# The last chunk's down projection: three float32r products of exact parts in place of seven float32 block products

## The chip, the cores and the metric

One NeuronCore of a Trainium2 chip runs the whole program. The metric is the device time of one execution in microseconds (us). Engines are named as in the profile: PE does the matmuls (PEld its weight loads), DVE, ACT and POOL are the vector, scalar and GpSimd engines, SP issues most of the DMAs. Each engine takes its instructions strictly in the order in which the kernel's Python emits them.

## The reference

An mLSTM cell runs over 768 steps of 4 batches and 8 heads of size 40; its output, laid out as 3072 tokens by 320 values, goes through a feed-forward block with an exact GELU. Cut to what matters here:

```
x = attn_out.transpose(0, 2, 1, 3).reshape(B * S, H * D)   # 3072 x 320
h = x @ w_in                                               # 320 x 2048
g = 0.5 * h * (1.0 + erf(h / sqrt(2)))
out = g @ w_out                                            # 2048 x 320
```

The weights come as float64 and everything is computed in float32.

## The kernel before

The sequence is cut into six chunks of 128 steps (`c` = 0 to 5). A chunk is 4 batches of 128 tokens, so 512 tokens. For each chunk there is the cell (scores, carried state, values), an up projection (`up`), and a down projection (`down_steps`). For c = 1 to 4 the down projection of chunk c is interleaved with the cell of chunk c+1, in an order written out by hand (the string `DOWN`: each `F` is one step of 16 matmuls of the down projection, other letters are steps of the cell). The last chunk, c = 5, has no cell beside it: its `up` and then its 14 `F` steps run alone.

**Up projection (L839 to L905).** The 2048 hidden values are 16 tiles `f` of 128; `HF` = 8, and tile f = 8e+i is named by e (0 or 1) and i. The product x·w_in is made of three float32r products: hi·hi, lo·lo and all·mid, where `w_in_hi`, `w_in_lo`, `w_in_mid` and `x_hi`, `x_lo`, `x_all` are exact parts of the factors (L703 to L720, L744 to L764); `PART` = 1 - 2^-13 and `BASE` = 1 + 2^-12 make the parts. The moving operand is 512 tokens wide. `pair(f)` (L845) makes two tiles i for both e, 24 matmuls over the first 256 rows of x, and `rest(u)` (L864) adds the last 64 rows for two pairs, 24 matmuls. The order is pair 0, pair 1, rest 0, pair 2, pair 3, rest 1. Pairs 0 and 2 write the PSUM buffers `h`,`h`,`a`,`a`; pairs 1 and 3 write `tr`,`tr`,`b`,`b`. `out` (L874) takes GELU on ACT from PSUM into `g`.

The parts hi and lo of w_in stay in SBUF; mid is summed anew in every chunk by `join_weight` (L762). Its results lie in two rings: joins 1, 4, 6 and 9 in the ring `pow` (two buffers, of which `T[4]`, a sum of w_out blocks, holds one from chunk 1 to its last use), the others in the ring `w_in` (12 buffers, of which the ten `w_in_lo` hold ten). Where a ring has no free buffer, the writer waits until the last reader of the oldest one is done. In `up`, DVE has these in order: joins 0, 1 (pair 0), 3, 4, 2 (pair 1), 5, 6, then, during pairs 2 and 3, 8, 9 and 7, between the sums of `hidden_sums`.

**Down projection (L934 to L999).** It is a Strassen-like scheme with seven block products in float32: blocks of 8 hidden tiles, 256 tokens and 160 output columns. `w_out` is held in SBUF as [128, 16, 320]; one block of it, `w_out[:, 0:8, 160:]`, is overwritten in chunk 1 by a difference of blocks (`weight_sum(3)`, `T[3]`), and `w_sums0`, `w_sums1` and `T[4]` hold further sums. Sums of `g` blocks are made by `hidden_sums` (L787) and, in the last chunk, `sum_late` (L974), both on DVE. Each product is 2 steps (token tiles t) of `HF` matmuls per tile, 128x128 weights and 160 moving columns; `p1` to `p7` evict them. The two products with `k == 3` have a bank for each token tile in the last chunk. `send` (L907) writes 128 tokens to DRAM in two DMAs; in the last chunk one of the two goes on ACT's queue.

**Buffers.** `const`, `raw`, `two`, `outp`, `wts`, `parts` (`fars[0]`) are SBUF pools, `gp` holds `g`, `ps_tr`, `ps_h`, `ps_mm` are PSUM pools of two buffers a tag. Tiles of one pool and tag share its buffers in turn.

Of the kernel before, what the change touches and what calls it, by code (L numbers as in the profile page):

```python
# [16 lines left out]
P = 128  # L17
# [19 lines left out]
DOWN = """  # L37
# [5 lines left out]
def kernel(  # L43
# [52 lines left out]

    w_out = const.tile([P, NF, DM], F32, name="w_out")
    ident = const.tile([P, P], F32, name="ident")  # L100
    e_hi = const.tile([P, 1], F32, name="e_hi")
    e_lo = const.tile([P, 1], F32, name="e_lo")
# [2 lines left out]
    ewT = const.tile([P, NCH - 1, BH], F32, name="ewT")  # L105
    gT = const.tile([P, NCH - 1, BH], F32, name="gT")
    dec = const.tile([P, NCH - 1, B * NP], F32, name="dec")
    state = [const.tile([P, NP, 2 * D1], F32, name=f"state{b}") for b in range(B)]
    blocks = const.tile([P, 2, H, DP], F32, name="blocks")
    qb = [blocks[:, n] for n in range(2)] + [const.tile([P, H, DP], F32, name="qb2")]  # L110
    by_block = blocks.rearrange("p n h d -> p (n h d)").rearrange("p (m i x) -> p m i x", m=NP, i=2)
    kb = [const.tile([P, H, DP], F32, name=f"kb{n}") for n in range(NQ)]
    vb = [const.tile([P, H, D1], F32, name=f"vb{n}") for n in range(NQ)]
    shared = lambda shape, dt, name: wts.tile(shape, dt, name=name, tag="hi", bufs=5)
    W = {n: shared([P, H, L], F32, f"W{n}") for n in range(B - 1)}
    qk = shared([P, 2, H, DP], F32, "qk")
    qb.append(qk[:, 0])
    kb.append(qk[:, 1])
    vb.append(shared([P, H, D1], F32, "v3"))
    ob = [const.tile([P, DM], F32, name=f"ob{n}") for n in range(NLD)]  # L120
    y_rest = const.tile([P, 2, R], F32, name="y_rest")
    last = gates.tile([P, P], F32, name="last")
    eye = gates.tile([P, P], BF16, name="eye")
# [2 lines left out]
    i_sb = gates.tile([BH, NCH, L], F32, name="i_sb")  # L126
    kq_d = [dram.tile([B, 2, H * L, D], F32, name=f"kq{c}_d") for c in range(2, NCH)]
    M_d = dram.tile([NCH - 1, BH, L], F32, name="M_d")
    swapped_d = [dram.tile([P, n, BH], F32, name=f"swapped{n}") for n in (NCH - 2, NCH - 3)]

    def out_of(n):
# [25 lines left out]
    def copy_chunk(c, batches=range(B)):  # L157

        for b in batches:
            for i, src in enumerate((k, q)):  # L160
                for hip in range(2):
                    nc.sync.dma_start(out=kq_d[c - 2][b, hip].rearrange("(m i x t) d -> i x m (t d)", m=NP, i=2, x=16)[i],
                                      in_=src[b, hip::2, c * L:(c + 1) * L, :].rearrange("m (x t) d -> x m (t d)", x=16))
# [572 lines left out]
    def products_begin():  # L736

        gate_ctx.close()
        pool = ctx.enter_context(tc.tile_pool(name="parts", bufs=1))
        w_sums.extend(pool.tile([P, HF, HD], F32, name=f"w_sums{n}") for n in range(2))  # L740
        parts["x_all"] = pool.tile([P, NX + 1, TG], F32R, name="x_all")
        fars.extend([pool])

# [18 lines left out]
    def join_weight(i):  # L762
        w_mid[i] = raw.tile([P, 2, WP // 2], F32R, name="w_in_mid", tag="pow") if i % 5 in (1, 4) else w_f(F32R, "w_mid")
        nc.vector.tensor_tensor(out=w_mid[i], in0=w_hi[i], in1=w_lo[i], op=OP.add)  # L764
# [22 lines left out]
    def hidden_sums(g, f0, f1):  # L787

        (a11, a21), (_, a22) = [[g.t[:, HF * e + f0:HF * e + f1, HT * h:HT * (h + 1)] for h in range(2)]
                                for e in range(2)]  # L790
        s1, s2 = [t[f0 // (HF // 2)][:, f0 % (HF // 2):f0 % (HF // 2) + f1 - f0, :] for t in (g.s1, g.s2)]
        nc.vector.tensor_tensor(out=s1, in0=a21, in1=a22, op=OP.add)  # L792
        nc.vector.tensor_tensor(out=s2, in0=s1, in1=a11, op=OP.subtract)
        nc.vector.tensor_tensor(out=a21, in0=a11, in1=a21, op=OP.subtract)
# [41 lines left out]

    def up(g, sums_too, turns):  # L839

        def split_to(i):
            while len(w_lo) <= i:
                split_weight()

        def pair(f, ahead):  # L845

            at = [f // 2 * 5 + f % 2 * 3 + x for x in range(NX)]
            split_to(at[1])
            for i in at:
                if i not in w_mid:  # L850
                    join_weight(i)
            pus = [[pool.tile([P, TG], F32, name="pu", tag=tag) for e in range(2)]
                   for pool, tag in (((ps_h, "h"), (ps_mm, "a")), ((ps_tr, "tr"), (ps_mm, "b")))[f % 2]]
            ahead()
            mid = [w_mid.pop(i) for i in at]
            for n, (w, x) in enumerate((([w_hi[i] for i in at], parts["x"]), ([w_lo[i] for i in at], parts["x_lo"]), (mid, parts["x_all"]))):
                for i in range(2):
                    for e in range(2):
                        for k in range(NX):
                            nc.tensor.matmul(in_pairs(pus[i][e]), w[k][:, e, i * P:(i + 1) * P], in_turns(x[:, k, :]),  # L860
                                             start=(n == 0 and k == 0), stop=False, skip_group_check=True)
            return pus

        def rest(u, banks, order):  # L864
            mid = w_mid.pop(5 * u + 2)
            for i in order:
                pu = banks[i]
                for n, (w, x) in enumerate(((w_hi[5 * u + 2], parts["x"]), (w_lo[5 * u + 2], parts["x_lo"]), (mid, parts["x_all"]))):
                    for e in range(2):
                        r = halves[e]  # L870
                        nc.tensor.matmul(in_pairs(pu[e]), w[r, i // 2, i % 2 * P:(i % 2 + 1) * P], in_turns(x[r, NX, :]), start=False,  # L871
                                         stop=(n == 2), skip_group_check=True)

        def out(i, e, pu):  # L874
            nc.scalar.activation(out=g.t[:, HF * e + i, :], in_=pu[e], func=AF.Gelu, scale=4097.0)  # L875

        if c == 1:
            copy_chunk(2, range(1, B))
        b0 = pair(0, lambda: split_to(4))
        b1 = pair(1, lambda: join_weight(2))  # L880
        for step in turns[:1]:
            step()
        while later_loads:
            later_loads.pop(0)()
        if c == 1:
            copy_chunk(3)
        rest(0, b0 + b1, (0, 1, 2, 3))
        split_to(6)
        join_weight(5)
        join_weight(6)  # L890
        for i, pu in enumerate(b0 + b1):
            for e in range(2):
                out(i, e, pu)
        for step in sums_too[:5]:
            step()
        b2 = pair(2, lambda: split_to(9))
        hidden_sums(g, 0, 2)
        b3 = pair(3, lambda: (hidden_sums(g, 2, 4), join_weight(7)))
        for step in turns[1:] + sums_too[5:]:
            step()  # L900
        rest(1, b2 + b3, (2, 3, 0, 1))
        for i, e in ((2, 0), (2, 1), (3, 0), (0, 0), (1, 0), (3, 1), (0, 1), (1, 1)):
            out(4 + i, e, (b2 + b3)[i])
        hidden_sums(g, HF - 2, HF)
        hidden_sums(g, HF - 4, HF - 2)  # L905
# [28 lines left out]
    def down_steps(c, g):  # L934
# [3 lines left out]

        def product(lhs, rhs, k, first, t, then):

            own = k == 3 and c == NCH - 1
            at, n, i = ((k, t), 1, 0) if own else (k, 2, t)
            if first and i == 0:
                bank[at] = ps_mm.tile([P, n, HD], F32, name="po", tag="a" if own else "b")
            for j in range(HF):

                nc.tensor.matmul(bank[at][:, i, :], lhs(j, t), rhs(j), start=(first and i == 0 and j == 0),  # L947
                                 stop=(i == n - 1 and j == HF - 1), skip_group_check=True)
            if own:
                then(bank[at], slice(t, t + 1))  # L950
            elif t == 1:
                then(bank[at])

        def block(h, n):
            if h not in o_sb:
# [12 lines left out]

        def p2(pb):
            nc.scalar.copy(out=block(0, 0), in_=pb)  # L970
            if c == NCH - 1:
                sum_late()

        def sum_late():  # L974
            for i in range(2):
# [3 lines left out]
        def p5(pb):  # L979
            add(block(1, 1), pb, block(1, 0))  # L980

        def p7(pb, tiles=slice(0, 2)):
            add(block(1, 1)[:, tiles], pb, block(1, 1)[:, tiles])

        def p3(pb):
            add(block(0, 1), pb, block(1, 0))
            for t in range(2):
                send(c, t, o_sb[0][:, t, :])

        def p4(pb, tiles=slice(0, 2)):  # L990
            add(block(1, 0)[:, tiles], pb, block(1, 0)[:, tiles])
            for t in range(2)[tiles]:
                send(c, 2 + t, o_sb[1][:, t, :])

        todo = ((A(0, 0), Bm[0][0], 0, True, p1), (Sm(g.s2), T[2], 1, True, p6),
# [39 lines left out]
    steps |= cell_steps(0, "mwgtscvyx") | cell_steps(1, "MWGTSCVYXR")  # L1035
    play(FRONT, steps)
    for c in range(1, NCH):
        g, later, steps = Hidden(True), [], {}
        if c + 1 < NCH:
            steps = cell_steps(c + 1, "MWGTscVYXRLKQDCBSjh", g)  # L1040
        up(g, weight_sum(1) + weight_sum(2) + weight_sum(3) if c == 1 else [], [lambda b=b: (steps["K"](b), steps["Q"](b)) for b in range(2)] if steps else [])
        if c == 1:
            later = weight_sum(4)
        products, late = down_steps(c, g)
        steps |= dict(F=in_turn(products), Z=in_turn(later), N=late)
        play("F " * 14 if c + 1 == NCH else DOWN, steps)


# [28 lines left out]
```

## Time and profile before

| | us |
|---|---|
| median of three runs | 470.47 (469.64, 470.47, 470.61) |
| the profiled execution, its own time | 470.64 |
| span of that execution | 468.8 |
| PE busy | 458.0 (98%) |
| DVE busy | 319.9 (68%) |
| ACT busy | 238.1 (51%) |
| last chunk's up projection on PE | 408.19 to 434.68 |
| last chunk's down projection on PE | 434.68 to 465.32 |

The span is from the first to the last instruction; the execution's own time is 1.8 us longer. "PEclk", the granted clock, is 1.00 in all of the stretches used here. An instruction's busy time includes its start and its drain, so that consecutive ones overlap: what an engine pays for one of many is the distance from start to start, read from the timeline, and not the mean of its busy time.

### The profile page before, as it was taken

Reading aid. Unit: us, or ns where it says so; the run is one execution under the profiler, and the core shown is the slowest. Engines: PE = TensorE matmul, PEld = TensorE weight load, DVE = VectorE, ACT = ScalarE, POOL = GpSimd, SP = SyncE. Lnnn points to the kernel's source line nnn. Section 1 sums busy time; section 2 is a strip of 40 time slices with the busy share of each in tenths; the row PEclk is TensorE's granted clock in tenths of the full one; section 3 lists DMA queues with packets and bytes.
Section 4 is the critical chain, followed back from the end, with each engine's and each line's share of the span. In section 5 each row is a group of like instructions: output and inputs, shape, how many; then the busy total and the mean of one; then the engine's idle time right before and its main releaser. Section 6 shows DMA issues by size and latency. Waiting matters only on the chain.

```text
span 468.8 us, 12989 instructions
## 1 busy us (share of the span) xinstructions
PE 458.0 (98%) x5380; PEld 406.4 (87%) x5380; DVE 319.9 (68%) x694; ACT 238.1 (51%) x517; POOL 79.8 (17%) x120
## 2 busy tenths in 40 slices
PE   8899999999999999999999999999999999999996
PEld 7787788867788899988898988899988899988996
DVE  7799879798878996746576645586646657624320
ACT  6886999954354684203783213684203883222300
POOL 3002120000020232300433200443203213000000
PEclk9899999999999999999999999999999999999999
DMA  9997993367876740067981056980059830100001
GB/s 174 190 198 178 201 232 87 86 127 202 142 189 121 116 80 3 24 117 154 196 131 17 22 119 141 209 133 14 30 79 216 121 78 1 37 23 0 1 1 56
DMA packets 172795, 49.80 MB, mean 106 GB/s; under 512 B 154720, under 2 KB 166272, under 8 KB 172736
## 3 DMA queue, kind: packets, MB, share of 16 engines
q1 hardware_dynamic: 172416, 48.64, 51.3%
q8 instruction: 42, 0.69, 0.6%
q10 hardware_dynamic: 320, 0.33, 0.2%
q14 instruction: 17, 0.14, 0.1%
HBM read 44.82 MB, written 9.37 MB: 116 GB/s over the span
## 4 chain that ended last, share of the span: by engine, by line
PE 87%; DVE 7%; DMA 2%; issue 1%; SPq 1%; ACT 1%; DVEq 0%
PE po L947 31%; PE pu L860 22%; PE po L924 7%; PE pu L871 6%; PE pu L805 5%; PE ph L656 3%; PE ps L554 2%; PE ps L538 2%; PE px L696 2%; PE pu L811 2%; PE pf L609 1%; DMA kb<-in_k_dram 1%; PE pf L620 1%; SPq L170 1%; PE pt L516 1%
## 5 line engine op out<-in xcount | busy, mean ns | idle before, releaser
L947 PE MATMUL po<-w_out,g 128*128 128x160 f32 x640 | 94.2, 302 | 0.0
L875 ACT ACTIVATE g<-pu 128x512 f32<-128x512 f32 x80 | 40.3, 620 | 98.3 <-PE pu L871 98.3
L947 PEld LDWEIGHTS po<-w_out,g 128*128 128x128 f32 x640 | 87.8, 190 | 2.5 <-ACT g L875 1.7
L947 PE MATMUL po<-w_sums,sums 128*128 128x160 f32 x320 | 45.9, 302 | 0.0
L947 PEld LDWEIGHTS po<-w_sums,sums 128*128 128x128 f32 x320 | 43.8, 190 | 0.4
L466 ACT ACTIVATE W<-W,aT 128x128 f32<-128x128 f32 x128 | 39.2, 389 | 2.0 <-POOL W L440 1.9
L860 PE MATMUL pu<-x_hi,w_in_hi 128*128 128x512 f32 x160 | 39.0, 386 | 0.0
L440 POOL TENSOR_SCALAR_AFFINE_SELECT W<-W 128x1024 f32<-128x1024 f32 (+2 forms) x20 | 24.7, 1245 | 81.6 <-DMA W<-M_d 81.1
L860 PE MATMUL pu<-x_lo,w_in_lo 128*128 128x512 f32 x160 | 37.8, 379 | 0.0
L924 PE MATMUL po<-w_out,g 128*128 128x320 f32 x128 | 35.2, 433 | 0.0
L960 DVE TENSOR_TENSOR o_sb<-po,o_sb 128x320 f32<-128x320 f32 (+1 forms) x27 | 12.5, 465 | 32.8 <-PE po L947 28.8
L860 PEld LDWEIGHTS pu<-x_hi,w_in_hi 128*128 128x128 f32 x160 | 29.6, 189 | 5.6 <-ACT g L875 1.7
L792 DVE TENSOR_TENSOR sums<-g 128x512 f32<-128x512 f32 x20 | 16.4, 820 | 26.5 <-ACT g L875 26.5
L860 PEld LDWEIGHTS pu<-x_lo,w_in_lo 128*128 128x128 f32 x160 | 30.2, 189 | 4.3
L525 POOL TENSOR_TENSOR vw<-vb,ewT 128x328 f32<-128x328 f32 x12 | 9.9, 837 | 137.8 <-DMA vb<-in_v_dram 97.8
L685 ACT COPY y_rest<-ob 128x128 f32<-128x128 f32 x16 | 4.8, 298 | 54.9 <-DVE ob L678 29.2
L924 PEld LDWEIGHTS po<-w_out,g 128*128 128x128 f32 x128 | 24.0, 190 | 9.6
L764 DVE TENSOR_TENSOR w_in_mid<-w_in_hi,w_in_lo 128x512 fp32r<-128x512 f32 x20 | 13.7, 687 | 24.4 <-PE pu L860 24.4
L860 PE MATMUL pu<-x_all,w_mid 128*128 128x512 f32 x80 | 30.3, 379 | 0.0
L860 PE MATMUL pu<-x_all,w_in_mid 128*128 128x512 f32 x80 | 30.3, 379 | 0.0
L805 PE MATMUL pu<-first_x,w_in 128*128 128x256 f32 x128 | 29.2, 382 | 0.6 <-DVE w_in L387 0.6
L805 PEld LDWEIGHTS pu<-first_x,w_in 128*128 128x128 f32 x128 | 23.8, 190 | 4.3 <-DVE w_in L387 1.0
(183 smaller groups left out, 879.3 us busy)
## 6 DMA issues: line engine op xcount, KB each, us to landing
W<-M_d SPq DMA_DIRECT2D x16, 512.0 KB, 5.5
bits<-in_moe_w_in_dram SPq DMA_DIRECT2D x20, 256.0 KB, 4.3
bits<-in_moe_w_out_dram SPq DMA_DIRECT2D x16, 320.0 KB, 3.2
blocks<-kq_d SPq DMA_DIRECT2D x32, 128.0 KB, 3.3
ob<-in_o_gate_dram SPq DMA_DIRECT2D x24, 160.0 KB, 3.9
out_dram<-o_sb SPq DMA_DIRECT2D x36, 80.0 KB, 2.0
kq_d<-in_k_dram SPq DMA_DIRECT2D x32, 80.0 KB, 2.6
kq_d<-in_q_dram SPq DMA_DIRECT2D x32, 80.0 KB, 2.4
```

The source lines that it names most:

```text
L440: nc.gpsimd.affine_select(out=x, in_=x, compare_op=OP.is_ge, fill=1.0e30, base=base, pattern=[[0, H], [1, x.shape[2]]], channel_multiplier=-1)
L466: nc.scalar.activation(out=W[n][:, h, :], in_=src, func=AF.Exp, scale=-1.0, bias=aT[:, self.c, r:r + 1])
L656: nc.tensor.matmul(ph[r, h, :], Pm[:, h, r], vb[turn_of(n)][:, h, :], start=True, stop=True)
L764: nc.vector.tensor_tensor(out=w_mid[i], in0=w_hi[i], in1=w_lo[i], op=OP.add)
L792: nc.vector.tensor_tensor(out=s1, in0=a21, in1=a22, op=OP.add)
L805: nc.tensor.matmul(banks[-1][e][:, i - i0, :], in_tile(i, x)[:, e, i % 2 * P:(i % 2 + 1) * P], first_x[:, x, t0:t1], start=(x == 0 and i = ...
L860: nc.tensor.matmul(in_pairs(pus[i][e]), w[k][:, e, i * P:(i + 1) * P], in_turns(x[:, k, :]), start=(n == 0 and k == 0), stop=False, skip_g ...
L871: nc.tensor.matmul(in_pairs(pu[e]), w[r, i // 2, i % 2 * P:(i % 2 + 1) * P], in_turns(x[r, NX, :]), start=False, stop=(n == 2), skip_group ...
L875: nc.scalar.activation(out=g.t[:, HF * e + i, :], in_=pu[e], func=AF.Gelu, scale=4097.0)
L924: nc.tensor.matmul(po[b], g.t[:, f, b * L:(b + 1) * L], w_out[:, f, :], start=(f == 0), stop=(f == NF - 1))
L947: nc.tensor.matmul(bank[at][:, i, :], lhs(j, t), rhs(j), start=(first and i == 0 and j == 0), stop=(i == n - 1 and j == HF - 1), skip_grou ...
L960: nc.vector.tensor_tensor(out=to, in0=pb, in1=x, op=OP.add)
```

## The change

The last chunk leaves the seven block products. A class `LastDown` forms, as the up projection does, three float32r products with the full width of 320 output columns: 4 token tiles, 16 hidden tiles and 3 kinds of part (hi, lo, all·mid). The parts of `w_out` are made in the last `up`: `weights` (hi, on ACT), `weights_lo` and `weights_mid` (on DVE). The parts of the hidden values are made per tile: `gelu` into a scratch tile, `split_hi` (ACT), `split_lo` (two DVE instructions). All of them lie in buffers that the last cell and the earlier chunks no longer use. The hidden tiles come in two rounds of eight (pairs 0 and 1; pairs 3 and 2). Since `w_out[:, 0:8, 160:]` is overwritten in chunk 1, that block is stored to DRAM before that, and loaded again in chunk 4 after `p7`, the last reader of the difference. The tags added to existing tiles only give the names by which their buffers are shared. Sums of `g` and `sum_late` are no longer made in the last chunk, and the special case `own` of `product` goes.

```
+    right_d = dram.tile([P, DFF // P // 2, DM // 2], F32, name="right_d")
...
+        ROUNDS = ((0, 8, 1, 9, 2, 10, 3, 11), (6, 14, 7, 15, 4, 12, 5, 13))
...
+            self.groups = [(0, 4, part(fars[0], "w_sums0", 4)), (8, 4, part(fars[0], "w_sums1", 4))]
+            singles = [part(const, f"{x}{n}") for x, m in (("ob", NLD), ("vb", NQ), ("state", B)) for n in range(m)]
+            singles += [part(two, "vw") for _ in range(2)] + [part(fars[0], "hs", bufs=2) for _ in range(2)]
+            triples = [part(wts, "W", 3) for _ in range(NW)]
+            singles += [x for t in triples for x in cut(t)]
+            self.groups += [(f, 1, singles.pop(0)) for f in (4, 12, 5, 13, 6, 14, 7, 15)]
...
+        def weights(self, f, n, to):
+            nc.scalar.activation(out=to, in_=w_out[:, f:f + n, :].rearrange("p f d -> p (f d)"), func=AF.Copy, scale=PART * 2.0 ** -12)
+        def weights_lo(self, f):
+            nc.vector.scalar_tensor_tensor(out=self.lo[f], in0=self.hi[f], scalar=-BASE * 2.0 ** 12, in1=w_out[:, f, :], op0=OP.mult, op1=OP.add)
+        def weights_mid(self, f):
+            if self.w_mid is None:
+                self.w_mid = const.tile([P, NF, DM], F32R, name="w_out_mid", tag="w_out")
+            nc.vector.tensor_tensor(out=self.w_mid[:, f, :], in0=self.hi[f], in1=self.lo[f], op=OP.add)
...
+        def gelu(self, f, pu):
+            n = len(self.whole) % HF
+            if n < 2:
+                if n == 0:
+                    self.two = const.tile([P, 2, TG], F32, name="g_whole", tag="blocks")
+                self.whole[f] = self.two[:, n, :]
+            else:
+                pool, tag = ((raw, "sig"), (outp, "o_sb"))[n // 2 % 2]
+                self.whole[f] = pool.tile([P, TG], F32, name="g_whole", tag=tag)
+            nc.scalar.activation(out=self.whole[f], in_=pu, func=AF.Gelu, scale=4097.0)
+        def split_hi(self, f):
...
+            nc.scalar.activation(out=self.b[f], in_=self.whole[f], func=AF.Copy, scale=PART)
+        def split_lo(self, f):
+            nc.vector.scalar_tensor_tensor(out=self.b_lo[f], in0=self.whole[f], scalar=-1.0 / BASE, in1=self.b[f], op0=OP.mult, op1=OP.add)
+            nc.vector.tensor_tensor(out=self.all[:, f, :], in0=self.whole[f], in1=self.b[f], op=OP.subtract)
+        def products(self):
+            po = [pool.tile([P, DM], F32, name="po", tag=tag) for pool, tag in ((ps_tr, "tr"), (ps_mm, "b")) for _ in range(2)]
+            part = lambda f: ((self.b[f], self.hi[f]), (self.b_lo[f], self.lo[f]), (self.all[:, f, :], self.w_mid[:, f, :]))
+            first, last = (self.ROUNDS[0][0], 0), (self.ROUNDS[1][-1], 2)
+            for n, ts in ((0, range(B)), (1, (0, 1)), (1, (2,)), (1, (3,))):
+                for k in range(3):
+                    for t in ts:
+                        for f in self.ROUNDS[n]:
+                            x, w = part(f)[k]
+                            nc.tensor.matmul(in_pairs(po[t]), x[:, t * L:(t + 1) * L], in_turns(w), start=(f, k) == first,
+                                             stop=(f, k) == last, skip_group_check=True)
+                for t in ts if n == 1 else ():
...
+                    nc.scalar.activation(out=o_sb[:, t % 2, :].rearrange("p (a i) -> p a i", a=2),
+                                         in_=po[t].rearrange("p (i a) -> p a i", a=2), func=AF.Copy, scale=4097.0)
+                    send(NCH - 1, t, o_sb[:, t % 2, :])
...
+    def up(g, sums_too, turns, last=None):
...
         if c == 1:
             copy_chunk(2, range(1, B))
+            nc.sync.dma_start(out=right_d, in_=w_out[:, 0:HF, HD:])
         b0 = pair(0, lambda: split_to(4))
         b1 = pair(1, lambda: join_weight(2))
+        if last:
+            for x in last.groups:
+                last.weights(*x)
+            for f in last.lo:
+                last.weights_lo(f)
...
         join_weight(5)
         join_weight(6)
+        if last:
+            for f in last.ROUNDS[0][0:4]:
+                last.weights_mid(f)
         for i, pu in enumerate(b0 + b1):
             for e in range(2):
                 out(i, e, pu)
+            if last:
+                for e in range(2):
+                    last.split_hi(HF * e + i)
...
         b2 = pair(2, lambda: split_to(9))
+        if last:
+            for f in last.ROUNDS[0][0:4]:
+                last.split_lo(f)
+        else:
+            hidden_sums(g, 0, 2)
+        b3 = pair(3, lambda: (last or hidden_sums(g, 2, 4), join_weight(7)))
+        if last:
+            for f in last.ROUNDS[0][4:]:
+                last.split_lo(f)
+            for f in last.ROUNDS[0][4:]:
+                last.weights_mid(f)
...
         rest(1, b2 + b3, (2, 3, 0, 1))
+        if last:
+            for f in last.ROUNDS[1]:
+                last.gelu(f, (b2 + b3)[f % HF - 4][f // HF])
+                last.split_hi(f)
+                last.split_lo(f)
+            for f in last.ROUNDS[1]:
+                last.weights_mid(f)
+            return
...
-            if c == NCH - 1:
-                sum_late()
...
+        def p7(pb):
+            add(block(1, 1), pb, block(1, 1))
+            if c == NCH - 2:
+                nc.sync.dma_start(out=w_out[:, 0:HF, HD:], in_=right_d)
...
+        if c + 1 == NCH:
+            down = LastDown()
+            up(None, [], [], down)
+            down.products()
+            break
```

More of the change, by code (lines that the diff above doesn't have):

```diff
@@ L94 @@
     ctx.enter_context(tc.manual_schedule())
-    w_out = const.tile([P, NF, DM], F32, name="w_out")
+    w_out = const.tile([P, NF, DM], F32, name="w_out", tag="w_out")
     ident = const.tile([P, P], F32, name="ident")
@@ L107 @@
     dec = const.tile([P, NCH - 1, B * NP], F32, name="dec")
-    state = [const.tile([P, NP, 2 * D1], F32, name=f"state{b}") for b in range(B)]
-    blocks = const.tile([P, 2, H, DP], F32, name="blocks")
-    qb = [blocks[:, n] for n in range(2)] + [const.tile([P, H, DP], F32, name="qb2")]
+    state = [const.tile([P, NP, 2 * D1], F32, name=f"state{b}", tag=f"state{b}") for b in range(B)]
+    blocks = const.tile([P, 2, H, DP], F32, name="blocks", tag="blocks")
+    qb = [blocks[:, n] for n in range(2)] + [const.tile([P, H, DP], F32, name="qb2", tag="qb2")]
     by_block = blocks.rearrange("p n h d -> p (n h d)").rearrange("p (m i x) -> p m i x", m=NP, i=2)
-    kb = [const.tile([P, H, DP], F32, name=f"kb{n}") for n in range(NQ)]
-    vb = [const.tile([P, H, D1], F32, name=f"vb{n}") for n in range(NQ)]
+    kb = [const.tile([P, H, DP], F32, name=f"kb{n}", tag=f"kb{n}") for n in range(NQ)]
+    vb = [const.tile([P, H, D1], F32, name=f"vb{n}", tag=f"vb{n}") for n in range(NQ)]
     shared = lambda shape, dt, name: wts.tile(shape, dt, name=name, tag="hi", bufs=5)
@@ L119 @@
     vb.append(shared([P, H, D1], F32, "v3"))
-    ob = [const.tile([P, DM], F32, name=f"ob{n}") for n in range(NLD)]
+    ob = [const.tile([P, DM], F32, name=f"ob{n}", tag=f"ob{n}") for n in range(NLD)]
     y_rest = const.tile([P, 2, R], F32, name="y_rest")
@@ L739, in products_begin @@
         pool = ctx.enter_context(tc.tile_pool(name="parts", bufs=1))
-        w_sums.extend(pool.tile([P, HF, HD], F32, name=f"w_sums{n}") for n in range(2))
+        w_sums.extend(pool.tile([P, HF, HD], F32, name=f"w_sums{n}", tag=f"w_sums{n}") for n in range(2))
         parts["x_all"] = pool.tile([P, NX + 1, TG], F32R, name="x_all")
@@ L833, in first_up, with __init__, places @@
         ups.clear()
-    def up(g, sums_too, turns):
+    class LastDown:
+        ROUNDS = ((0, 8, 1, 9, 2, 10, 3, 11), (6, 14, 7, 15, 4, 12, 5, 13))
+        def __init__(self):
+            self.all = gp.tile([P, NF, TG], F32R, name="g_all", tag="g")
+            self.hi, self.lo, self.w_mid = {}, {}, None
+            self.b, self.b_lo, self.whole, self.places_of = {}, {}, {}, {}
+            part = lambda pool, tag, n=1, **kw: pool.tile([P, n * DM], F32R, name="w_out_part", tag=tag, **kw)
+            cut = lambda t: [t[:, i:i + DM] for i in range(0, t.shape[1], DM)]
+            self.groups = [(0, 4, part(fars[0], "w_sums0", 4)), (8, 4, part(fars[0], "w_sums1", 4))]
[4 more added lines that the diff above has]
+            self.groups += [(f, 1, singles.pop(0)) for f in (4, 12, 5, 13, 6, 14, 7, 15)]
+            for f, n, t in self.groups:
+                self.hi.update(zip(range(f, f + n), cut(t)))
+            self.lo = dict(zip((0, 1, 2, 3, 8, 9, 10, 11, 4, 12, 5, 13, 6, 14, 7, 15), singles))
+        def weights(self, f, n, to):
[6 more added lines that the diff above has]
+            nc.vector.tensor_tensor(out=self.w_mid[:, f, :], in0=self.hi[f], in1=self.lo[f], op=OP.add)
+        def places(self, n):
+            row = lambda pool, tag, k=1, **kw: [t[:, i, :] for t in [pool.tile([P, k, TG], F32R, name="g_part", tag=tag, **kw)] for i in range(k)]
+            if n == 0:
+                old = [x for tag in ("kT", "qT", "kT", "qT") for x in row(two, tag)]
+                old += [x for tag in ("kb0", "kb1", "kb2", "qb2") for x in row(const, tag)]
+                return old + [x for _ in range(NB) for x in row(raw, "bits", 2, bufs=NB)]
+            old = [x for _ in range(2) for x in row(wts, "hi", 2, bufs=5)] + [x for _ in range(5) for x in row(wts, "w_in", bufs=12)]
+            return old + [x for tag, pool in (("x", raw), ("x_lo", fars[0])) for x in row(pool, tag, 3, bufs=1)] + row(wts, "w_in", bufs=12)
+        def gelu(self, f, pu):
+            n = len(self.whole) % HF
+            if n < 2:
+                if n == 0:
+                    self.two = const.tile([P, 2, TG], F32, name="g_whole", tag="blocks")
[5 more added lines that the diff above has]
+        def split_hi(self, f):
+            n = int(f not in self.ROUNDS[0])
+            if n not in self.places_of:
+                self.places_of[n] = self.places(n)
+            i = self.ROUNDS[n].index(f)
+            self.b[f], self.b_lo[f] = self.places_of[n][i], self.places_of[n][HF + i]
+            nc.scalar.activation(out=self.b[f], in_=self.whole[f], func=AF.Copy, scale=PART)
[6 more added lines that the diff above has]
+            first, last = (self.ROUNDS[0][0], 0), (self.ROUNDS[1][-1], 2)
+            o_sb = None
+            for n, ts in ((0, range(B)), (1, (0, 1)), (1, (2,)), (1, (3,))):
[6 more added lines that the diff above has]
+                for t in ts if n == 1 else ():
+                    if t % 2 == 0:
+                        o_sb = outp.tile([P, 2, DM], F32, name="o_sb", tag="o_sb")
+                    nc.scalar.activation(out=o_sb[:, t % 2, :].rearrange("p (a i) -> p a i", a=2),
+                                         in_=po[t].rearrange("p (i a) -> p a i", a=2), func=AF.Copy, scale=4097.0)
+                    send(NCH - 1, t, o_sb[:, t % 2, :])
@@ L875, in out @@
             nc.scalar.activation(out=g.t[:, HF * e + i, :], in_=pu[e], func=AF.Gelu, scale=4097.0)
+        if last:
+            out = lambda i, e, pu: last.gelu(HF * e + i, pu[e])
         if c == 1:
             copy_chunk(2, range(1, B))
+            nc.sync.dma_start(out=right_d, in_=w_out[:, 0:HF, HD:])
         b0 = pair(0, lambda: split_to(4))
         b1 = pair(1, lambda: join_weight(2))
+        if last:
[3 more added lines that the diff above has]
+                last.weights_lo(f)
         for step in turns[:1]:
@@ L896, in up @@
         b2 = pair(2, lambda: split_to(9))
-        hidden_sums(g, 0, 2)
-        b3 = pair(3, lambda: (hidden_sums(g, 2, 4), join_weight(7)))
+        if last:
[9 more added lines that the diff above has]
+                last.weights_mid(f)
         for step in turns[1:] + sums_too[5:]:
@@ L901, in up @@
         rest(1, b2 + b3, (2, 3, 0, 1))
+        if last:
+            for f in last.ROUNDS[1]:
[5 more added lines that the diff above has]
+            return
         for i, e in ((2, 0), (2, 1), (3, 0), (0, 0), (1, 0), (3, 1), (0, 1), (1, 1)):
@@ L939, in product @@
         def product(lhs, rhs, k, first, t, then):
[L941 to L944, printed above, removed]
+            if first and t == 0:
+                bank[k] = ps_mm.tile([P, 2, HD], F32, name="po", tag="b")
             for j in range(HF):
[L947 to L952, printed above, removed]
+                nc.tensor.matmul(bank[k][:, t, :], lhs(j, t), rhs(j), start=(first and t == 0 and j == 0),
+                                 stop=(t == 1 and j == HF - 1), skip_group_check=True)
+            if t == 1:
+                then(bank[k])
         def block(h, n):
@@ L980, in p5 @@
             add(block(1, 1), pb, block(1, 0))
-        def p7(pb, tiles=slice(0, 2)):
-            add(block(1, 1)[:, tiles], pb, block(1, 1)[:, tiles])
+        def p7(pb):
+            add(block(1, 1), pb, block(1, 1))
+            if c == NCH - 2:
+                nc.sync.dma_start(out=w_out[:, 0:HF, HD:], in_=right_d)
         def p3(pb):
@@ L988, in p3, with p4 @@
                 send(c, t, o_sb[0][:, t, :])
-        def p4(pb, tiles=slice(0, 2)):
-            add(block(1, 0)[:, tiles], pb, block(1, 0)[:, tiles])
-            for t in range(2)[tiles]:
+        def p4(pb):
+            add(block(1, 0), pb, block(1, 0))
+            for t in range(2):
                 send(c, 2 + t, o_sb[1][:, t, :])
@@ L1037 @@
     for c in range(1, NCH):
[L1038 to L1041, printed above, removed]
+        if c + 1 == NCH:
[3 more added lines that the diff above has]
+            break
+        g, later = Hidden(True), []
+        steps = cell_steps(c + 1, "MWGTscVYXRLKQDCBSjh", g)
+        up(g, weight_sum(1) + weight_sum(2) + weight_sum(3) if c == 1 else [], [lambda b=b: (steps["K"](b), steps["Q"](b)) for b in range(2)])
         if c == 1:
@@ L1045 @@
         steps |= dict(F=in_turn(products), Z=in_turn(later), N=late)
-        play("F " * 14 if c + 1 == NCH else DOWN, steps)
+        play(DOWN, steps)
 _INS = ['q', 'k', 'v', 'i_gate', 'f_gate', 'o_gate', 'moe_w_in', 'moe_w_out']
```

## The prediction

> **What bounds the kernel now.** First the engines' shares, then the chain that ended last over the last chunk (start, length, engine and line).
>
> ```profile
> PE 458.0 (98%) x5380; PEld 406.4 (87%) x5380; DVE 319.9 (68%) x694; ACT 238.1 (51%) x517; POOL 79.8 (17%) x120
> ...
> 408.19 10.36 PE pu L860 x48
> 418.55 2.79 PE pu L871 x24
> 421.34 10.56 PE pu L860 x48
> 431.90 2.79 PE pu L871 x24
> 434.68 30.64 PE po L947 x224
> 465.32 0.02 issue
> 465.35 0.33 DVE o_sb L960
> ```
>
> From 408.19 to 465.32 PE never waits: whatever PE is spared there is gained, as long as nothing new makes it wait. The float32 products take 30.64/224 = 0.137 us each for 160 columns (0.86 ns a column); the float32r products of the up projection 10.36/48 = 0.216 us for 512 (0.42 ns a column).
>
> The timelines of DVE, ACT and SP say what room there is (start, busy time, line, operation, idle time before it).
>
> ```profile
> 398.09 0.49 DVE L678 TENSOR_TENSOR ob<-ob,den 128x320 f32<-128x320 f32 x1 [0.59 <-POOL ob L673]
> 398.50 0.48 DVE L960 TENSOR_TENSOR o_sb<-po,o_sb 128x320 f32<-128x320 f32 x1
> ...
> 408.63 0.68 DVE L764 TENSOR_TENSOR w_mid<-w_in_hi,w_in_lo 128x512 fp32r<-128x512 f32 x1
> 409.23 0.69 DVE L764 TENSOR_TENSOR w_in_mid<-w_in_hi,w_in_lo 128x512 fp32r<-128x512 f32 x1
> 409.84 0.69 DVE L764 TENSOR_TENSOR w_mid<-w_in_hi,w_in_lo 128x512 fp32r<-128x512 f32 x1
> 413.41 0.69 DVE L764 TENSOR_TENSOR w_in_mid<-w_in_hi,w_in_lo 128x512 fp32r<-128x512 f32 x1 [2.89 <-PE pu L860]
> 414.02 0.68 DVE L764 TENSOR_TENSOR w_mid<-w_rest_hi,w_in_lo 128x512 fp32r<-128x512 f32 x1
> ```
> ```profile
> 132.59 2.18 ACT L756 ACTIVATE w_in_hi<-w_in 128x512 fp32r<-128x512 f32 x4
> ...
> 406.56 1.28 ACT L875 ACT_TABLE_LOAD   x1
> 419.43 4.03 ACT L875 ACTIVATE g<-pu 128x512 f32<-128x512 f32 x8 [11.59 <-PE pu L871]
> ```
> ```profile
> 379.55 1.28 SPq L152 DMA_DIRECT2D vb<-in_v_dram  x2
> 403.77 62.39 SPq L914 DMA_DIRECT2D out_dram<-o_sb  x12
> ```
>
> Two paces follow. DVE: 512-wide two-input instructions start 0.605 us apart, 320-wide ones 0.41. ACT: a GELU (4.03-0.62)/7 = 0.49, a copy of 512 (2.18-0.64)/3 = 0.51, one of 320 by its width 0.35, of 1280 1.15; where an instruction needs the one just before it, 0.66. The joins at 408.63 to 414.02 are 0, 1, 3, 4 and 2: join 4 waited for the end of PE's pair 0 (413.37). SP issues nothing from 380.8 to 403.8.
>
> **PE's part.** 224 x 0.137 = 30.64 go, 4 x 16 x 3 = 192 products of 320 columns come. None such is in the trace. Nearest are the rows above: 320 columns at the float32r rate are 0.135 us, and 160 columns at half that rate are 0.137, with weight loads of the same size. I take 0.136: 26.1 us, a gain of 4.5. The far bounds are the weight load's busy time (mean 0.190) and the float32 rate (320 x 0.86 = 0.274).
>
> **ACT's part.** `weights`: 2 x 1.15 + 8 x 0.35 = 5.1 us, from 406.6 (end of the last x part) to 411.7, then the table load to 413.0: hidden, the first GELU can't start before 419.43. Then 8 GELUs and 8 copies a round. In round 0 these alternate by two, so the second GELU pair (f = 1, 9) ends at 422.0 and 422.5 where before it ended at 421.0 and 421.5; pair 2 needs its buffers at 422.2 and 422.6. It just fits.
>
> **DVE's part, step by step.** Added: 16 lows and 16 mids of w_out (32 x 0.41 = 13.1 us) and 32 splits of hidden tiles (32 x 0.605 = 19.4). DVE is in order, so these run when the joins let them. `T[4]` has had its last reader at 408.19, so join 4 finds a second `pow` buffer and runs at 410.4. Join 2 doesn't gain: ring `w_in` has 12 buffers, ten held by `w_in_lo`, two by joins 0 and 3, so it waits for pair 0's end, 413.41. Behind it stands everything: 16 lows to 420.57, joins 5 and 6 to 421.78 (needed at 424.8), 4 mids to 423.42, then splits of f = 0, 8, 1, 9, ending at 424.6, 425.8, 427.05 and 428.26.
>
> Here is the **new wait**. GELU of f = 3 and 11 writes the two `o_sb` buffers that f = 1 and 9 occupy until their splits end. So these GELUs end at about 427.8 and 429.0 instead of 423. They empty the PSUM buffers `b`, which pair 3 needs from its fifth matmul on: due at 426.5 + 4 x 0.216 = 427.4, starting at 427.9 (0.5 late), and two matmuls later due at 428.3, starting at 429.1 (0.8 late). **PE loses 1.3 us** and the up projection ends at 436.0.
>
> After that DVE has: joins 8, 9, 7 to 430.1 (9 needed at about 431.3), splits to 434.9, mids to 436.6, round 1's splits to 446.2, mids to 449.5. PE asks for round 0's lows at 440.4 and mids at 444.7; for round 1's hi at 449.1 (ACT ends 443.4), lows at 451.2, mids at 453.4. All covered, the last by 3.9 us; beyond that each us that DVE is late is a us lost. The PSUM banks `tr` and `b` are free by GELUs of f = 6, 14, 7, 15 in time (1 us or more).
>
> What goes from DVE (four groups of hidden sums, `sum_late`, seven adds) is off the path except the last add: 0.33 becomes an ACT copy of 0.43, so +0.1.
>
> **The DMAs.** The reload (655 KB, pieces of 640 bytes) stands on SP ahead of the sends at 403.8; it can start when the last matmul of `T[3]` ends, 397.6. The row of most bytes is
>
> ```profile
> W<-M_d SPq DMA_DIRECT2D x16, 512.0 KB, 5.5
> ```
>
> so 5.5 to 6.9 us: landed by 404.5, before ACT wants it at 406.6; up to 412.8 it costs nothing. The store in chunk 1 goes ahead of the loads of `blocks` at 143.1, which are used at 155.4 and would have landed by 149.2: 6 us to spare against 5.5 to 6.9. Taken as 0, bounds 0 and 2.
>
> **Sum.** -4.5 + 1.3 + 0.1 = -3.1 us on the span of 468.8 (465.7) and on that execution's 470.64 (467.5). It was 0.17 above the median of the runs, 470.47; from that the forecast is 467.4.
>
> **Rivals.**
> (A) The forecast, 467.4 (466.4 to 468.4): 0.50.
> (B) No stall in pair 3: 467.4 - 1.3 = 466.1. It needs DVE about 1.3 us earlier, as if join 2 had a free buffer (it would run at 411.0). For it: join 5 ran at 414.6 in this chunk, so buffers come free sooner than in the others; against: that is after pair 0. 0.13.
> (C) DVE instructions don't overlap and cost their whole busy time, 0.69 and 0.49. Then the 16 lows, two joins, 4 mids and eight splits push the end of split 9 by 2.5 us; the stall is 3.7, not 1.3: 469.8. Against: the joins above start 0.60 apart at 0.69 busy. For: each new one waits for ACT, and waits may break the overlap. 0.14. The Trainium skill (VectorE: DVE Perf Modes, section The DRAIN you can't avoid) has this as its rule: a next instruction does not begin before the pipe of the one ahead is empty. The trace of before disagrees by 0.08 us an instruction; by the rule the sum would be this 469.8.
> (D) The slower one: DVE's pace falls below its busy time.
>
> ```profile
> 133.36 0.68 DVE L758 SCALAR_TENSOR_TENSOR w_in_lo<-w_rest_hi,w_rest 128x512 fp32r<-128x512 f32 x1
> 134.15 1.49 DVE L758 SCALAR_TENSOR_TENSOR w_in_lo<-w_in_hi,w_in 128x512 fp32r<-128x512 f32 x2
> ```
>
> The same operation as a low starts 0.79 apart here, two of them and the next. At 0.79 and 0.57 all 64 new ones cost 11 us more; pair 3 then waits 6.3 us, and the last mids come 2.5 us too late: 467.4 + 5.0 + 2.5 = 474.9. The gain is gone from 0.72 and 0.51 on. For it: half of the new ones are of this kind. Against: these had waits on several engines, and an instruction for the wait between them; the new ones wait for ACT only. 0.09.
> (E) The 320-column products go at the weight load's 0.19: 192 x 0.054 = 10.4 more, 477.8; no gain from 0.152 on. Against: the 160-column ones load the same weights at 0.137. 0.06.
> (F) Store or reload comes late: up to 3 us, about 469 (467.4 to 470.4). 0.08.
>
> **Range and chances.** A, B, C and F hold 0.85; from 465.6 (B less 0.5) to 470.6 (C and F's ends). D and E stay outside. About 0.2% (0.94 us) can be told from no change: faster is below 469.5, slower above 471.4. Faster: A and B whole, a third of C, half of F: 0.72. Same: the rest of C and most of F's, 0.11. Slower: D, E and the tails, 0.17.
>
> **What would show it.** In the timeline of the changed kernel: 192 matmuls 0.136 apart (E if not); join 2 at 413.4 and lows 0.41 apart behind it (B, C, D by their pace); a gap of 1.3 us in PE within pair 3, ended by ACT's GELU, which waited for DVE; no gap in the products; the reload landed before 406. I am wrong if PE waits in the products or if chunks 1 to 4 take longer than before.

## The result and the profile after

| | before | after |
|---|---|---|
| median of the runs taken together, us | 469.11 (7 runs) | 465.95 (7 runs) |
| ratio of the two | | 0.9933, 95% interval 0.9909 to 0.9957 |
| profiled execution, its own time | 470.64 | 465.24 |
| span | 468.8 | 463.2 |
| last up projection and products on PE | 408.19 to 465.32: 57.13 | 406.84 to 459.65: 52.81 |

The kernel is faster by 0.67%; 3.2 us by the medians, 2.0 to 4.3 by the interval. The engines' shares of the changed kernel, and its chain that ended last over the last chunk:

```profile
PE 452.3 (98%) x5348; PEld 400.5 (86%) x5348; DVE 336.7 (73%) x737; ACT 253.0 (55%) x545; POOL 79.0 (17%) x120
...
406.84 10.36 PE pu L949 x48
417.20 2.79 PE pu L960 x24
419.99 10.58 PE pu L949 x48
430.57 2.79 PE pu L960 x24
433.36 26.29 PE po L919 x192
459.65 0.02 issue
459.67 0.44 ACT o_sb L924
```

The products take 26.29 us instead of 30.64, and the two pairs 2 and 3 together 10.58, where they took 10.56: the wait of 1.3 us that was forecast within pair 3 isn't there. The chain is PE's from end to end, as before.

DVE's timeline from join 4 to the split of f = 9 (start, busy time, line, operation, idle time before):

```profile
409.08 0.69 DVE L765 TENSOR_TENSOR w_in_mid<-w_in_hi,w_in_lo 128x512 fp32r<-128x512 f32 x1
410.11 0.69 DVE L765 TENSOR_TENSOR w_mid<-w_rest_hi,w_in_lo 128x512 fp32r<-128x512 f32 x1 [0.34 <-PE pu L949]
410.72 6.51 DVE L867 SCALAR_TENSOR_TENSOR w_out_part<-w_out_part,w_out 128x320 fp32r<-128x320 f32 x16
...
423.58 0.69 DVE L905 SCALAR_TENSOR_TENSOR g_part<-g_whole,g_part 128x512 fp32r<-128x512 f32 x1
424.18 0.68 DVE L906 TENSOR_TENSOR g_all<-g_whole,g_part 128x512 fp32r<-128x512 f32 x1
```

Join 4 (409.08) no longer waits. Join 2 waits 0.34 us and starts at 410.11, that is 3.27 us after pair 0 began, and not 5.22 as forecast; the split of f = 9 (the last two lines) ends 2 us sooner than I had it. The pace is the one taken: 0.60 for 512, and 16 lows in 6.51, 0.40 apart. On ACT the GELU of f = 11 still waits for that split, but shortly, and nobody waits for it:

```profile
424.96 0.60 ACT L893 ACTIVATE g_whole<-pu 128x512 f32<-128x512 f32 x1 [0.25 <-DVE g_all L906]
```

It ends at 425.56; pair 3 began at 425.23, and needs this buffer at its seventh matmul, 425.23 + 6 x 0.216 = 426.5. So 1.0 us is to spare. The reload, from SP's timeline and from the row of DMA issues (KB, us to landing):

```profile
396.25 0.57 SPq L1099 DMA_DIRECT2D w_out<-right_d  x1
...
w_out<-right_d SPq DMA_DIRECT2D x1, 640.0 KB, 5.0
```

It had landed by about 401.8, 3.3 us before ACT's first copy of w_out at 405.09.

### The profile page after: what moved, and what is told of

Its sections match the earlier page's. It is cut to its first block, busy times and chain, and to the rows that moved or that the text cites. A ratio compares the mean times of both kernels' runs of the same rounds, so it can differ in the third digit from the quotient of the medians.

```text
span 463.2 us, 13002 instructions
## 1 busy us (share of the span) xinstructions
PE 452.3 (98%) x5348; PEld 400.5 (86%) x5348; DVE 336.7 (73%) x737; ACT 253.0 (55%) x545; POOL 79.0 (17%) x120
## 4 chain that ended last, share of the span: by engine, by line
PE 89%; DVE 4%; DMA 2%; SPq 1%; POOL 1%; issue 1%; ACT 0%; DVEq 0%; POOLq 0%
PE po L1065 25%; PE pu L949 23%; PE po L1044 7%; PE pu L806 6%; PE pu L960 6%; PE po L919 6%; PE ph L657 4%; PE ps L555 3%; PE pu L812 2%; PE px L697 2%; PE pf L610 1%; PE ps L539 1%; SPq L155 1%; PE pf L577 1%; PE pt L517 1%
## 5 line engine op out<-in xcount | busy, mean ns | idle before, releaser
L1065 PE MATMUL po<-w_out,g 128*128 128x160 f32 x512 | 76.2, 303 | 0.0
L964 ACT ACTIVATE g<-pu 128x512 f32<-128x512 f32 x64 | 32.2, 618 | 77.4 <-PE pu L960 77.4
L1065 PEld LDWEIGHTS po<-w_out,g 128*128 128x128 f32 x512 | 70.3, 190 | 2.2 <-ACT g L964 1.3
L1065 PE MATMUL po<-w_sums,sums 128*128 128x160 f32 x256 | 36.9, 302 | 0.0
L1065 PEld LDWEIGHTS po<-w_sums,sums 128*128 128x128 f32 x256 | 35.0, 190 | 0.4
L1044 PEld LDWEIGHTS po<-w_out,g 128*128 128x128 f32 x128 | 24.0, 190 | 9.6
L793 DVE TENSOR_TENSOR sums<-g 128x512 f32<-128x512 f32 x16 | 13.6, 853 | 18.3 <-ACT g L964 18.3
L561 DVE TENSOR_TENSOR W<-ps,W 128x256 f32<-128x256 f32 (+1 forms) x48 | 17.9, 413 | 10.7 <-PE ps L555 9.0
```

Source lines behind the costliest of these rows:

```text
L561: nc.vector.tensor_tensor(out=w[r, :, t], in0=ps[i][hip][r, :, t], in1=w[r, :, t], op=OP.mult)
L1044: nc.tensor.matmul(po[b], g.t[:, f, b * L:(b + 1) * L], w_out[:, f, :], start=(f == 0), stop=(f == NF - 1))
L1065: nc.tensor.matmul(bank[k][:, t, :], lhs(j, t), rhs(j), start=(first and t == 0 and j == 0), stop=(t == 1 and j == HF - 1), skip_group_che ...
```

## The experiments

**The gain again.** The changed kernel unaltered, in two further series against the one before.

> The changed kernel once more, against the one before in five rounds. Theory (the gain is PE's: 30.64 us of products become 26.29, less 0.1 at the end): a gap of 4.2 us between the medians, ratio 0.991. Rival (the rest of the program pays back about 1 us, by the store and reload or by more DMA traffic): 3.1 us, ratio 0.9934.

> The changed kernel a third time, beside the next two on one chip. Theory (noise of about 1 us between series): 465 to 466 us, and within 0.5 us of the kernel without store.

Medians: 465.22 against 468.57 (ratio 0.9925, 0.9897 to 0.9954), and 464.63 against 468.02 (0.9917, 0.9888 to 0.9947). So the medians differ by 3.2, 3.4 and 3.4 us in the three series: less than the 4.2 expected of the second, and nearer to its rival's 3.1. The third median, 464.63, lies just below the 465 to 466 expected. The products took 26.29 us in each of the three profiles, and pairs 2 and 3 together 10.57 or 10.58. The last stretch is 4.32 us shorter, 4.25 with the end of the span; that is still within the interval of each series, in the first one just (4.27). What the medians lack, 0.9 us, is taken up below.

**Do store and reload cost?** Both left out, and then the reload alone (`# ...` says in which run a line goes; with `no_store` the declaration of `right_d` goes too):

```
-            nc.sync.dma_start(out=right_d, in_=w_out[:, 0:HF, HD:])      # no_store only
...
-            if c == NCH - 2:
-                nc.sync.dma_start(out=w_out[:, 0:HF, HD:], in_=right_d)  # no_store and store_only
```

> The changed kernel without the store of the block of w_out in chunk 1 and without its reload in chunk 4 (the last chunk then computes with the overwritten block). Theory (both are hidden): the same time as the changed kernel, within 0.5 us, and the same 69.0 us from the first to the second up projection. Rival (they cost): 1 us or more faster than the changed kernel.

> The kernel without store and reload again (the last chunk computes with the overwritten block). Theory (hidden): within 0.5 us of the changed kernel. Rival (store or reload cost 1 us, as the first pair of medians, 464.22 and 465.22, would have it): 1 us faster again.

> With the store in chunk 1, without the reload in chunk 4 (the last chunk computes with the overwritten block). Theory: as the changed kernel. Rival (the store costs): as the changed kernel, with no_store_2 1 us faster. Other rival (the reload costs): as no_store_2.

First series: 464.22 without them, 465.22 with them, which looked like the rival. Second series, all three on one chip: 464.70 without, 464.30 with the store alone, 464.63 with both. The 1 us doesn't come again. From the first to the second up projection all took the same: 69.05 and 69.04 us without the store, 69.04, 69.04 and 69.03 in the three profiles with it, 69.04 in the kernel before. Chunk 4, with the reload at its end, takes 67.41 to 67.43 us with it and without it. So both transfers are hidden in the chunks in which they run.

They aren't quite free all the same, for they show outside the span. The execution's own time is 1.74 to 1.84 us longer than its span in all 33 executions of the kernel before whose spans were taken. In the 19 of the changed kernel it is 1.82 to 2.11 longer, 1.99 in the mean; with the store alone 1.96 (12 executions), without both 1.83 (12). So about 0.2 us of the gain in the span doesn't reach the execution's time, and 0.16 of that goes when store and reload are left out. Why, no run here shows.

**Is the rest of the gap between 4.3 and 3.3 us in the part ahead?** The kernel before, profiled twice more.

> The kernel before, profiled again. Theory (what lies ahead of the last up projection varies from one execution to the next and is the same in both kernels): the last up projection starts between 404.5 and 408.2 us and takes, with the products, 57.1 us. Rival (the changed kernel pays about 1 us ahead of it): the start lies below 404.5.

> The kernel before once more. Theory (the part ahead of the last up projection is the same in both kernels and varies): a start between 404.5 and 408.2 us. Rival (the changed kernel pays about 1 us there): below 404.5.

Its last up projection starts at 405.75 and 405.12 (408.19 in the first profile). In the seven profiles of kernels that share the changed kernel's earlier part it starts between 404.57 and 408.04, 406.55 in the mean, against 406.35 in the mean of the three of before. What varies is the start of the program (the first up projection of a chunk begins at 128.5 to 131.3) and chunks 2 and 3 together (137.9 to 141.7 us); chunk 4 takes 67.41 to 67.43 in all.

The start goes by the granted clock. The windows from 16 to 18 us of `before` and of `after` (us, then busy time and count of PE, PEld, DVE, ACT and POOL, then the granted clock, DMA share, GB/s):

```profile
16.00:18.00 2.00, 2.00 (x19) 1.75 (x18) 0.51 (x2) 1.97 (x6) 0.00 (x0) 0.50 1.23 170
16.00:18.00 2.00, 2.00 (x25) 1.50 (x22) 1.43 (x4) 1.97 (x6) 0.00 (x0) 1.00 1.12 163
```

Four of the thirteen profiles (`before`, `before_b`, `after_third`, `no_store_2`) have 0.50 there, and in these the first up projection starts at 130.0 to 131.3; in the nine with 1.00 it starts at 128.5 to 129.2. The difference is 1.9 us in the mean. It comes in both kernels, and the profile from which the forecast was made had it.

Chunks 2 and 3 took 140.7 us in the mean of the eight profiles with the store (139.4 to 141.7), and 139.4 in the mean of the five without it, the kernel before among them (137.9 to 140.2). A loss of the missing size could lie there, but the two ranges overlap, and the medians of the second series above (464.70 without the store, 464.30 and 464.63 with it) have no such difference. It is not shown.

The last stretch of the kernel before is 57.13 us in all three profiles.

**Join 2 made to wait as forecast.** In the last chunk (`rest_late` is filled just ahead of it) join 2 gets a buffer of the ring `pow`, which join 1 holds until the end of pair 0:

```
-        ... tag="pow") if i % 5 in (1, 4) else w_f(F32R, "w_mid")
+        ... tag="pow") if i % 5 in (1, 4) or (i == 2 and rest_late) else w_f(F32R, "w_mid")
```

> In the last chunk join 2 is put into the ring pow, so that it has to wait for the end of pair 0 as the prediction had it. Theory (the predicted chain join 2 -> splits of f = 1 and 9 -> GELU of f = 3 and 11 -> buffers b -> pair 3 is right, only its start was misplaced): join 2 starts 5.2 us after pair 0 begins instead of 3.3, and PE loses about 1.3 us within pair 3. Rival (the chain has more slack than I gave it): no gap in pair 3.

DVE's timeline, and then the chain that ended last, from the split of f = 9 on:

```profile
407.85 0.68 DVE L766 TENSOR_TENSOR w_in_mid<-w_in_hi,w_in_lo 128x512 fp32r<-128x512 f32 x1
410.81 0.69 DVE L766 TENSOR_TENSOR w_in_mid<-w_rest_hi,w_in_lo 128x512 fp32r<-128x512 f32 x1 [2.29 <-PE pu L950]
```
```profile
424.36 0.60 DVE g_part L906
424.96 0.61 DVE g_all L907
425.58 0.02 issue
425.60 0.02 ACTq L894
425.62 0.04 issue
425.66 0.61 ACT g_whole L894
426.27 0.04 issue
426.31 4.15 PE pu L950 x18
430.46 2.79 PE pu L961 x24
433.25 26.29 PE po L920 x192
```

Join 2 starts 5.2 us after pair 0 began (405.60). Now the chain leaves PE: the split of f = 9 ends, GELU of f = 11 runs, and only then come the last 18 matmuls of pair 3. From the start of the up projection to the products it is 27.65 us against 26.52: 1.1 us lost, 1.3 forecast. The chain is shown; its start was what I had wrong. (The whole execution took 465.16 us. The part ahead varies by more than this loss, so it is read from the stretch alone.)

**DVE loaded further.** The lows are made twice:

```
-            for f in last.lo:
+            for f in list(last.lo) * 2:
```

> The 16 lows of w_out are made twice (the second time with the same values): 6.5 us more of DVE's work, before everything that DVE does for the hidden tiles. Theory (DVE's slack is about 0.1 us for pair 3 and about 5 us for the products): pair 3 waits about 5.5 us, the products don't wait. Rival (DVE isn't near the path): under 1 us in all.

The up projection to the products took 33.83 us instead of 26.52, so 7.3 us were lost, more than the 5.5 expected; the products took 26.29 without a gap. The whole execution took 472.18 us. PE's timeline over pairs 2 and 3, then busy times and granted clock by stretch (us, then busy time and count of PE, PEld, DVE, ACT and POOL, then the granted clock, DMA share, GB/s):

```profile
423.95 0.48 PE L949 MATMUL pu<-x_all,w_mid 128*128 128x512 f32 x1 [0.67 <-DVE w_mid L765]
...
426.16 1.03 PE L949 MATMUL pu<-x_hi,w_in_hi 128*128 128x512 f32 x4
430.46 0.70 PE L949 MATMUL pu<-x_hi,w_in_hi 128*128 128x512 f32 x2 [3.27 <-ACT g_whole L893]
431.66 0.73 PE L949 MATMUL pu<-x_hi,w_in_hi 128*128 128x512 f32 x2 [0.51 <-ACT g_whole L893]
432.20 3.58 PE L949 MATMUL pu<-x_lo,w_in_lo 128*128 128x512 f32 x8
```
```profile
426.20:432.20 6.00, 2.23 (x10) 1.32 (x8) 6.00 (x11) 1.79 (x4) 0.00 (x0) 1.00 0.00 0
432.20:435.60 3.40, 3.40 (x10) 2.68 (x9) 3.40 (x6) 0.44 (x1) 0.00 (x0) 0.50 0.00 0
```

Three parts. Pair 2 waits for joins 5 and 6 (0.67 and more: its last third should have begun at 423.1, and the pair ends 1.3 late); this I hadn't counted. Pair 3 waits for the GELUs: its fifth matmul was due at 426.16 + 4 x 0.216 = 427.0 and came at 430.46, its ninth was due at 427.9 and came at 432.2, 4.3 late in all. And then PE's clock is granted at half: eight matmuls take 3.40 us, 1.7 more than at 1.00. Together 1.3 + 4.3 + 1.7 = 7.3.

**The order of reading, and the width.** Token tiles 2 and 3 read the weights in order instead of alternating between the halves of a row (the copy out of PSUM follows suit; the order of writing into PSUM is the same); and, in another kernel, these tiles' products of round 1 are cut into two of 160.

```
-   nc.tensor.matmul(in_pairs(po[t]), x[...], in_turns(w), ...)
+   nc.tensor.matmul(in_pairs(po[t]) if t < 2 else po[t], x[...], in_turns(w) if t < 2 else w, ...)    # contig
...
+   cuts = (slice(0, HD),) if n == 0 or t < 2 else (slice(0, HD // 2), slice(HD // 2, HD))             # narrow
+   for m in cuts:
+       nc.tensor.matmul(in_pairs(po[t])[:, m, :], x[...], in_turns(w)[:, m, :], ...)
```

> For token tiles 2 and 3 the products read the moving weights in order, column by column, instead of alternating between the two halves of the row; tiles 0 and 1 stay as they are. Theory (a float32r product costs its 320 columns at one rate, in whatever order they are read): 0.137 us from start to start for all tiles. Rival (the alternating read is what gives the rate, or what costs a little): tiles 2 and 3 go at another pace, 0.27 us at the float32 rate.

> In round 1, for token tiles 2 and 3, each product of 320 columns is made as two of 160 with the same weights loaded each time (48 matmuls become 96). Theory (the weight load, 0.19 busy, is far from binding at 320 columns and binds at 160): the pair costs more than 0.137, at 0.19 each 18.2 us instead of 6.6. Rival (loads are hidden wholly even at 160 columns): 0.069 each, the same 6.6 us.

PE's timelines, of the first (round 1: tiles 0 and 1 in the first two lines, tile 2 in the next two), then of the second (tile 2, then the start of tile 3):

```profile
444.70 4.51 PE L919 MATMUL po<-w_out_part,g_part 128*128 128x320 f32 x32
449.05 2.34 PE L919 MATMUL po<-w_out_mid,g_all 128*128 128x320 f32 x16
451.22 2.51 PE L919 MATMUL po<-w_out_part,g_part 128*128 128x320 f32 x16
453.57 1.33 PE L919 MATMUL po<-w_out_mid,g_all 128*128 128x320 f32 x8
454.74 2.52 PE L919 MATMUL po<-w_out_part,g_part 128*128 128x320 f32 x16
```
```profile
453.44 3.69 PE L921 MATMUL po<-w_out_part,g_part 128*128 128x160 f32 x32
456.98 1.95 PE L921 MATMUL po<-w_out_mid,g_all 128*128 128x160 f32 x16
458.76 3.74 PE L921 MATMUL po<-w_out_part,g_part 128*128 128x160 f32 x32
```

Alternating: (451.22 - 444.70)/48 = 0.136 a product. In order: (454.74 - 451.22)/24 = 0.147, 8% slower; the products as a whole took 27.35 us. So the alternating read gives a little, and neither expectation held (0.137, and 0.27). Cut in two: (458.76 - 453.44)/48 = 0.111 a product, 0.222 for the pair, between the two expectations (0.19 and 0.069 a product). At the rate of the 512-column products, 0.42 ns a column, 160 columns are 0.067 us, so something other than the columns bounds these products. It may be the load of 128 by 128 weights that each has ahead of it, as the expectation had it, but no run takes the two apart. In any case 0.111 is below the 0.19 that a load is busy, and below 0.136, so at 320 columns it doesn't show. The two executions took 464.06 and 469.69 us.

## Why the prediction was right, and where not

- **PE's part** held: 26.29 for 26.1 us; a product costs 0.136 and the whole is 4.35 shorter, 4.5 forecast. Rival E (0.19 a product) is refuted; even the products of 160 columns, with the same loads, cost 0.111.
- **The new wait in pair 3** was the step that failed: "it waits for pair 0's end, 413.41". In the last chunk `w_in_lo` 0 has its last reader in pair 0's 15th matmul, and then its buffer in the ring is free for good. The chain of the kernel with the lows made twice has that release in so many words (start, length, engine and line):

```profile
406.46 3.25 PE pu L949 x15
409.71 0.02 issue
409.73 0.04 DVE w_mid L765
```

  So join 2 came 1.95 us earlier and the wait of 1.3 vanished, with 1.0 us to spare. In the kernel before, this was hidden behind join 4, which stood ahead of join 2 and did wait for pair 0's end. The rest of the chain (splits, `o_sb`, GELU, buffers `b`, pair 3) is right: with join 2 delayed as forecast, 1.1 us were lost. What happened is thus rival B's case, which I gave 0.13, and against which I had argued that the buffers come free only after pair 0.
- **DVE's pace** held: 0.60 and 0.40, where 0.605 and 0.41 were taken. Rivals C and D are refuted, for the new instructions too, whose wait for ACT was over. The rule of the Trainium skill that rival C names (VectorE: DVE Perf Modes, The DRAIN you can't avoid) doesn't describe them: they start 0.60 apart at 0.68 busy. The same section of the Trainium skill adds, which the prediction left out, that a next instruction which isn't held back starts earlier; the trace fits that.
- **ACT's part** held: ten copies in 5.30 us (5.1), GELU and copy 1.15 us a tile in round 1 (0.66 + 0.51).
- **The end** held: from the last product to the end of the span 3.55 us, 3.48 before (+0.1 forecast).
- **Store and reload** held within the span: landed after 4.0 and 5.0 us, where 5.5 to 6.9 were taken, and hidden, so rival F is refuted. The 0.2 us outside the span weren't foreseen.
- **The sum.** Forecast -3.1 with the wait, -4.4 without; the last stretch shows -4.3 and, with the end, -4.25, the medians -3.2 to -3.4. That the medians lie nearer to the forecast is no merit of the step that failed. Of the missing 0.9 us, 0.2 lie outside the span, where the prediction let the span's gain pass whole into the execution's time. Whether the rest is noise of the part ahead of the last chunk, or a small loss there, stays open: the intervals hold both. The time of 465.95 lies 1.5 below the forecast 467.4; 1.36 of that is that the median of before, too, came out lower over seven runs than over three (469.11 for 470.47).

## What to carry to other kernels

On an engine that never waits, a change is worth the products that it drops, provided that the engines that prepare the parts hand them over in time; walk their queues in order, and ask for every buffer when its last reader is done in this very pass, not in the usual one: in the last pass buffers come free sooner. A wait that one sees may hide, behind it in the queue, another that ends earlier. And a long wait of PE can cost more than its length: in the one run with a wait of 3.3 us, the clock stood at half for 3.4 us behind it.

## What the runs showed of the hardware

- After a wait of 3.3 us and one of 0.5 close behind it (`lows_twice`), PE's granted clock was 0.50 for 3.4 us, which cost 1.7 us more; it was still 1.00 for the first 1.7 us after the longer wait. Waits of 1.1 us in all had no such effect (`join2_late`). The Trainium skill (TensorE: Matmul & The Clock Gate, Part 1: The HAM clock gate) has the half rate after an idle window of about 3.4 us; this trace agrees in the rate, and nearly in the length of the wait (3.27 us).
- The half rate came without a long wait, too. In four of the thirteen profiles the clock stood at 0.50 from 16 to 18 us. In `before` this lasted from about 15.4 to 18.8, and in the 5 us ahead of it no wait of PE is longer than 0.4 us. Why in these four, no run here shows.
- A float32r product of 320 columns takes 0.136 us if the moving operand alternates between two places in the row, and 0.147 if it is read in order. Why, no run here shows.
- With 160 columns it takes 0.111, not half of 0.136.
